# Seven of 32 zero regions in packets of 14 KiB, with a wider zero tile and the room for it, in a decode attention and FFN backward kernel

## Chip, cores and metric

One core of one Trainium2 chip. The metric is device time in microseconds, the median of several executions.

## The reference, cut to what matters

The reference computes one decode step of attention over the last 4096 keys of a long cache, a gated FFN, and the gradients of everything.

```python
W = min(4096, max(256, Sk // 4))              # 4096 of Sk = 32768
k = repeat(k_cache[:, :, Sk - W:, :], rep)    # B=2, Hkv=8, Dh=128, rep=4
v = repeat(v_cache[:, :, Sk - W:, :], rep)
p = softmax(q @ k.T * Dh ** -0.5)
h = x + (p @ v).reshape(B, 1, Hq * Dh) @ wo
out = h + (gelu(ln(h) @ w_gate) * (ln(h) @ w_up)) @ w_down
# returned: out and the gradients of x, k_cache, v_cache, wq, wo, w_gate, w_up, w_down
```

The gradients of the two caches are zero outside the last 4096 rows. These zeros are 32 regions (two tensors, two batches, eight heads) of 7 MiB each, 234.88 MB, and the kernel has to write them.

## The kernel before, where the change touches it

The zeros go out on GpSimd's queue from a u8 tile of 2048 columns. The DMA widens its bytes, so that a packet is 8 KiB of output (29376 packets for 234.88 MB on the page of the kernel before). (Three dots stand for further lines.)

```python
ZE = 2048
zt = const.tile([P, ZE], U8)
zero_regions = [...]                          # 32 regions of 7 MiB
ZPK = Z * DH // 2 // ZE
def zero_cast(i):
    dst, done = zero_regions[i].bitcast(F32), 0
    for rows, n in ZERO_PARTS.get(i, ((P, ZPK // P),)):
        ...
        nc.gpsimd.dma_start(out=..., in_=src.unsqueeze(1).to_broadcast([rows, n, ZE]))
...
nc.gpsimd.tensor_scalar(out=zt[:], in0=wq_sb[:, 0, 0:ZE // 2].bitcast(U8),   # after wq has landed
                        scalar1=0, scalar2=None, op0=ALU.mult)
for i in range(len(zero_regions)):
    zero_cast(i)
```

Attention of a batch runs over eight groups of heads. While VectorE and TensorE work on the products of group g (`m_unit`), TensorE transposes the K tile of group g+1 and computes its scores. There is one PSUM buffer for scores, below called the score bank:

```python
def s_unit(g, u, KT):
    if u == 0:
        S_ps[g] = ps_A.tile([P, NJ, REP], F32, tag="S", name="S_ps")   # pool with bufs=1
    ...
def softmax(g):
    S = S_ps.pop(g)
    ...                                                                # row maximum, negated
    ef = stA.tile([P, NJ, REP], F32, tag="ef", name="ef", bufs=1)
    ee = stA.tile([P, NJ, REP, 2], BF16, tag="ee", name="ee")
    nc.vector.tensor_tensor(out=ef[:], in0=S[:], in1=negm..., op=ALU.add)          # L394
    nc.scalar.activation(out=ef[:], in_=ef[:], func=ACT.Exp)                       # L395
    nc.vector.tensor_copy(out=ee[:], in_=ef[:].unsqueeze(3)...)                    # L396
    nc.vector.tensor_copy(out=eT[:]..., in_=ef[:]...)                              # L398
    nc.vector.reduce_sum(out=lsum[:, 0, ...], in_=ef[:]..., axis=AX.X)             # L400
```

In the lines of the profile PE is TensorE, DVE is VectorE, ACT is ScalarE, POOL is GpSimd, and SP is SyncE, which issues the loads and stores.

## Time and profile before

| | kernel before |
|---|---|
| the six executions known before the prediction | median 792.12 us, 791.67 to 796.31 |
| all 111 executions of this study | median 792.63, mean 793.5; 77 under 793.5, 11 at 798 or over |
| span of the profiled execution | 797.6 us |

The kernel ran again later (run e1); its profile there has a span of 790.2 us, and I use that one, called "the usual run" below, to compare with. The DMA rate in its forty slices of the span:

```profile
GB/s 364 420 417 421 419 426 427 422 430 427 429 422 418 426 423 423 426 424 430 429 428 428 429 427 426 429 422 428 428 428 430 423 422 421 424 419 423 422 381 367
```

The last two slices read 381 and 367 GB/s, where the profile that the prediction shows has 236 and 356. In a usual run the DMA engines work to the end.

### The profile page before, as it was taken

To read this page: it belongs to the slowest core of one execution; us is meant where nothing else is said; L and a number is where in the kernel's file an instruction comes from. 1 tells how busy PE (TensorE), PEld (TensorE's weight loads), DVE (VectorE), ACT (ScalarE), POOL (GpSimd) and SP (SyncE) were. 2 spreads that over 40 slices of the span, in tenths; PEclk is the share of its full clock that TensorE was granted. 3 is DMA by queue.
4 is the path that set the end of the run, shared out by engine and by line. 5 is a ranking of instruction groups with operands and counts; after the bars stand their busy time and mean duration, and the time that the engine had idled before them with its cause. 6 is when DMAs were issued, how large, how long until landed. Compare 5 with 4: busy or idle time off the path is not lost.

```text
span 797.6 us, 12388 instructions
## 1 busy us (share of the span) xinstructions
PE 563.4 (71%) x5032; PEld 302.5 (38%) x5096; DVE 474.0 (59%) x1161; ACT 280.9 (35%) x406; POOL 40.5 (5%) x58
## 2 busy tenths in 40 slices
PE   3899997787687998830837969988697733681072
PEld 3655653445555554410415444534242210220020
DVE  1699998137434898750821386755636944992093
ACT  1534330135245342100201343635443641682063
POOL 4300000000000000000000000000000000000000
PEclk9999999777699999885966868955586785996577
DMA  8999999999999999999999999999999999999968
GB/s 367 417 418 423 417 426 428 422 429 428 427 421 420 424 424 426 425 425 431 427 429 429 427 428 426 427 424 429 428 426 431 422 421 422 422 420 422 421 236 356
DMA packets 40986, 332.44 MB, mean 417 GB/s; under 512 B 2000, under 2 KB 2016, under 8 KB 2144
## 3 DMA queue, kind: packets, MB, share of 16 engines
q0 software_dynamic: 29376, 234.88, 77.0%
q1 hardware_dynamic: 11540, 96.75, 49.4%
q8 instruction: 40, 0.66, 0.3%
q10 hardware_dynamic: 12, 0.01, 0.2%
q14 instruction: 18, 0.15, 0.0%
HBM read 49.30 MB, written 282.33 MB: 416 GB/s over the span
## 4 chain that ended last, share of the span: by engine, by line
PE 22%; DMA 14%; DVE 8%; ACT 4%; issue 2%; SPq 1%; ACTq 0%; DVEq 0%
DMA out_dram<-mem 12%; PE ps_gr L713 3%; ACT mem L93 3%; PE ps_tb L240 3%; PE VT_ps L642 3%; PE ps_g L822 2%; DVE mem L91 2%; PE dP_ps L651 2%; DMA mem<-in_A_x_dram 2%; DVE junk L586 2%; PE ps_gq L793 1%; PE d_ln_ps L770 1%; PE attn_ps L516 1%; PE d_ln_ps L571 1%; DVE mem L733 1%
## 5 line engine op out<-in xcount | busy, mean ns | idle before, releaser
L408 DVE TENSOR_TENSOR mem<-mem,ee 128x512 bf16<-128x512 bf16 x512 | 181.0, 422 | 41.9 <-PE KT_ps L364 30.7
L419 PE MATMUL M_ps<-mem 128*128 128x512 bf16 x468 | 135.2, 390 | 9.2 <-DVE mem L408 6.1
L93 ACT CAST mem<-ps_g 128x512 bf16<-128x512 f32 x128 | 74.2, 585 | 88.9 <-PE ps_g L822 82.9
L822 PE MATMUL ps_g<-mem 128*128 128x512 bf16 x250 | 81.1, 417 | 21.4 <-DVE mem L91 14.0
L366 ACT COPY mem<-KT_ps 128x1024 bf16<-128x1024 bf16 x64 | 63.2, 1013 | 82.3 <-PE KT_ps L364 78.3
L91 DVE CAST mem<-ps_g 128x512 bf16<-128x512 f32 x128 | 82.6, 687 | 7.1 <-ACT mem L93 5.1
L364 PE MATMUL KT_ps<-ident_bf,mem 128*128 128x128 bf16 x512 | 45.9, 233 | 32.8 <-DMA mem<-in_A_k_cache_dram 29.5
L113 POOL DMA_DIRECT2D out_dram<-zt x38 | 32.4, 997 | 665.1 <-DMA out_dram<-zt 664.8
L240 PE MATMUL ps_tb<-ident_bf,mem 128*128 128x128 bf16 x480 | 56.3, 251 | 9.9 <-DMA mem<-in_B_w_gate_dram 3.2
L419 PEld LDWEIGHTS <-mem 128*128 128x128 bf16 x512 | 43.5, 99 | 48.3 <-issue 14.4
L822 PEld LDWEIGHTS <-mem 128*128 128x128 bf16 x256 | 26.0, 103 | 76.3 <-issue 57.0
L93 ACT COPY mem<-ps_tb 128x512 bf16<-128x512 bf16 x44 | 25.8, 585 | 74.9 <-PE ps_tb L240 70.1
L240 PEld LDWEIGHTS <-mem 128*128 128x128 bf16 x480 | 37.5, 128 | 35.5 <-issue 30.8
L364 PEld LDWEIGHTS <-mem 128*128 128x128 bf16 x512 | 34.5, 104 | 40.3 <-DMA mem<-in_A_k_cache_dram 30.0
L642 PE MATMUL VT_ps<-ident_bf,mem 128*128 128x128 bf16 x512 | 47.2, 241 | 2.9 <-ACT mem L93 1.1
L642 PEld LDWEIGHTS <-mem 128*128 128x128 bf16 x512 | 37.0, 108 | 28.1 <-issue 21.2
L651 PE MATMUL dP_ps<-mem 128*128 128x512 bf16 x114 | 41.1, 437 | 4.6 <-ACT mem L93 4.5
L93 ACT COPY mem<-VT_ps 128x1024 bf16<-128x1024 bf16 x31 | 31.7, 1022 | 35.2 <-PE VT_ps L642 34.0
L91 DVE COPY mem<-ps_tb 128x512 bf16<-128x512 bf16 x44 | 18.7, 424 | 42.0 <-PE ps_tb L240 40.6
L713 PE MATMUL ps_gr<-mem 2*128 2x512 bf16 (+1 forms) x78 | 33.6, 496 | 12.8 <-DVE mem L733 7.4
L261 PE MATMUL ps_rows<-ident_bf,mem 128*128 128x128 bf16 x4 | 1.1, 287 | 58.0 <-DVE mem L260 58.0
L91 DVE CAST mem<-ps_gr 128x512 bf16<-128x512 f32 (+1 forms) x38 | 24.8, 656 | 27.6 <-PE ps_gr L713 27.6
(242 smaller groups left out, 631.7 us busy)
## 6 DMA issues: line engine op xcount, KB each, us to landing
out_dram<-zt POOLq DMA_DIRECT2D x31, 7168.0 KB, 165.0
out_dram<-mem SPq DMA_DIRECT2D x36, 1024.0 KB, 28.9
mem<-in_A_k_cache_dram SPq DMA_DIRECT2D x16, 1024.0 KB, 23.1
mem<-in_A_v_cache_dram SPq DMA_DIRECT2D x16, 1024.0 KB, 22.5
out_dram<-mem SPq DMA_DIRECT2D x5, 1792.0 KB, 18.9
out_dram<-zt POOLq DMA_DIRECT2D x1, 5040.0 KB, 124.0
mem<-in_A_wq_dram SPq DMA_DIRECT2D x1, 4096.0 KB
mem<-in_A_wo_dram SPq DMA_DIRECT2D x1, 4096.0 KB, 31.4
```

Of the source, the lines that this page charges most:

```text
L91: nc.vector.tensor_copy(out=out, in_=in_)
L93: nc.scalar.copy(out=out, in_=in_)
L113: nc.gpsimd.dma_start(out=dst[done * ZE:(done + rows * n) * ZE].rearrange("(p k e) -> p k e", p=rows, k=n), in_=src.unsqueeze(1).to_broadc ...
L240: nc.tensor.transpose(out=ps[:, a, :], in_=src_block(a), identity=ident_bf[:])
L364: nc.tensor.transpose(out=KT_ps[:, jj, :], in_=Kt[b, g][:, u * 8 + jj, :], identity=ident_bf[:])
L366: nc.scalar.copy(out=KT[:], in_=KT_ps[:])
L408: nc.vector.tensor_tensor(out=pk[:, :, i, :].rearrange("p j (d t) -> p j d t", t=2), in0=Kb[:, j0:j0 + pk_j, :].rearrange("p j (d t) -> p ...
L419: nc.tensor.matmul(out=M_ps[:], lhsT=Vt[b, g][:, j, :], rhs=pk[:, jj, :, :].rearrange("p i d -> p (i d)"), start=(j == 0), stop=(j == NJ - 1))
L642: nc.tensor.transpose(out=VT_ps[:, jj, :], in_=Vt[b, g][:, a * 8 + jj, :], identity=ident_bf[:])
L651: nc.tensor.matmul(out=dP_ps[:, c, :], lhsT=dOpad[:, w0:w0 + P], rhs=VT[:, c * 4:(c + 1) * 4, :].rearrange("d a k -> d (a k)"), start=(i = ...
L713: nc.tensor.matmul(out=ps[:, :n], lhsT=lhsT_fn(k), rhs=rhs_fn(k), start=True, stop=True)
L822: nc.tensor.matmul(out=ps[:, a2, :], lhsT=lhs_bf[:, jp * P:(jp + 1) * P], rhs=rhs_bd[:, ap * 2 + a2, gq * 4:(gq + 1) * 4, :].rearrange("q ...
```

## The change

The intent is to save time in the seven regions written while no load or store runs, by fewer packets, of 14 KiB. This needs a zero tile of 3584 columns, and the other edits make its 1536 bytes per partition free.

```diff
-    ZE = 2048
+    ZE = 3584
     zt = const.tile([P, ZE], U8)
-    ZPK = Z * DH // 2 // ZE
+    ZE_BIG = (4, 5, 6, 17, 18, 19, 20)
     def zero_cast(i):
+        ze = ZE if i in ZE_BIG else 2048
+        zpk = Z * DH // 2 // ze
...
-    dqT_hb = small.tile([P, HQ, B], BF16)
...
-                ef = stA.tile([P, NJ, REP], F32, tag="ef", name="ef", bufs=1)
+                ef = S
...
+             tc.tile_pool(name="mid", bufs=1) as mid:
-            dO2 = small.tile([P, NOR], F32, name=f"dO2_{b}", tag="dO2")
+            dO2 = mid.tile([P, NOR], F32, name=f"dO2_{b}", tag="dO2")
-            dq_f32 = small.tile([P, HQ], F32, name=f"dq_f32_{b}", tag="dq_f32")
+            dq_f32 = mid.tile([P, HQ], F32, name=f"dq_f32_{b}", tag="dq_f32")
-            nc.scalar.activation(out=dqT_hb[:, :, b], in_=dq_f32[:], func=ACT.Copy, scale=SCALE)
...
-            nc.tensor.matmul(out=d_ln1_ps[:]..., lhsT=dqT_hb[:, h, :], ...)
+            nc.tensor.matmul(out=d_ln1_ps[:]..., lhsT=dqT_bf[:, h::HQ], ...)
```

More of the change, by code (lines that the diff above doesn't have):

```diff
@@ L99 @@
     dVv = out_3[:, :, Z:, :].rearrange("b g (p j) d -> p b g j d", p=P)
-    ZE = 2048
+    ZE = 3584
     zt = const.tile([P, ZE], U8)
     zero_regions = [o[b, g, 0:Z, :].rearrange("r d -> (r d)") for o in (out_2, out_3) for b in range(B) for g in range(HKV)]
-    ZPK = Z * DH // 2 // ZE
-    ZERO_PARTS = {i: ((4, 1), (15, 2), (2, 2), (15, 42), (12, 3), (P, 1), (16, 4)) for i in (30,)}
+    ZE_BIG = (4, 5, 6, 17, 18, 19, 20)
+    ZERO_PARTS = {30: ((4, 1), (15, 2), (2, 2), (15, 42), (12, 3), (P, 1), (16, 4))}
     def zero_cast(i):
         dst, done = zero_regions[i].bitcast(F32), 0
-        for rows, n in ZERO_PARTS.get(i, ((P, ZPK // P),)):
-            src = zt[0:rows * (P // rows):P // rows, :]
-            nc.gpsimd.dma_start(out=dst[done * ZE:(done + rows * n) * ZE].rearrange("(p k e) -> p k e", p=rows, k=n),
-                                in_=src.unsqueeze(1).to_broadcast([rows, n, ZE]))
+        ze = ZE if i in ZE_BIG else 2048
+        zpk = Z * DH // 2 // ze
+        for rows, n in ZERO_PARTS.get(i, ((P, zpk // P),)):
+            src = zt[0:rows * (P // rows):P // rows, 0:ze]
+            nc.gpsimd.dma_start(out=dst[done * ze:(done + rows * n) * ze].rearrange("(p k e) -> p k e", p=rows, k=n),
+                                in_=src.unsqueeze(1).to_broadcast([rows, n, ze]))
             done += rows * n
-        assert done == ZPK
+        assert done == zpk
     dh2_x = at(OFF_XR, [98, D], BF16, "xr")
@@ L505, in middle @@
         with tc.tile_pool(name="ps_W", bufs=2, space=PSUM) as ps_W, \
-             tc.tile_pool(name="ps_B", bufs=1, space=PSUM) as ps_B:
+             tc.tile_pool(name="ps_B", bufs=1, space=PSUM) as ps_B, \
+             tc.tile_pool(name="mid", bufs=1) as mid:
             attn_ps = ps_B.tile([B, D], F32)
@@ L769, in use_q @@
         def use_q(h, wqT_h):
-            nc.tensor.matmul(out=d_ln1_ps[:].rearrange("b a p -> b (a p)"), lhsT=dqT_hb[:, h, :],
+            nc.tensor.matmul(out=d_ln1_ps[:].rearrange("b a p -> b (a p)"), lhsT=dqT_bf[:, h::HQ],
                              rhs=wqT_h[:].rearrange("d a p -> d (a p)"), start=(h == 0), stop=(h == HQ - 1))
```

## The prediction

> **What bounds the kernel now.** I read the DMA rows of the page first, then the queue table, then the chain of work that ended last, then single stretches.
>
> The page's slices and its queue table:
>
> ```profile
> DMA  8999999999999999999999999999999999999968
> GB/s 367 417 418 423 417 426 428 422 429 428 427 421 420 424 424 426 425 425 431 427 429 429 427 428 426 427 424 429 428 426 431 422 421 422 422 420 422 421 236 356
> DMA packets 40986, 332.44 MB, mean 417 GB/s; under 512 B 2000, under 2 KB 2016, under 8 KB 2144
> q0 software_dynamic: 29376, 234.88, 77.0%
> q1 hardware_dynamic: 11540, 96.75, 49.4%
> ```
>
> The DMA engines run at 417 to 431 GB/s in all slices but the first and the last two. q0 is the zero fill: 234.88 MB in 29376 packets is 8.0 KB each (2048 bytes of the u8 zero tile, widened to 8192 bytes of output). q1 is everything useful, 96.75 MB. So the zeros are 71% of the bytes and fill whatever the loads and stores leave free. A first reading is "bandwidth-bound: any gain in the rate is a gain in time". The two low slices, 758 to 797 us, speak against that. The chain of work that ended last there:
>
> ```profile
> 638.17 30.30 DMA out_dram<-mem
> ...
> 690.00 26.33 DMA out_dram<-mem
> 716.35 40.67 DMA out_dram<-mem
> 757.99 1.10 issue
> 759.09 2.37 DVE mem L271 x2
> ```
>
> The busy table of stretches (length, busy us of PE, PEld, DVE, ACT and POOL, granted clock, DMA share, GB/s):
>
> ```profile
> 628.00:758.00 130.00, 57.95 (x184) 18.58 (x185) 70.56 (x109) 53.75 (x93) 2.04 (x3) 0.75 1.16 422
> ...
> 762.00:770.00 8.00, 6.71 (x21) 2.27 (x20) 6.69 (x11) 5.46 (x10) 0.00 (x0) 0.74 0.56 210
> 770.00:776.00 6.00, 5.19 (x19) 1.70 (x18) 5.53 (x10) 5.13 (x10) 0.00 (x0) 1.00 0.26 109
> ```
>
> The last of the four dK/dV jobs can build its block-diagonal operand (L271) only at 757.99 us, when a store that had 40.67 us to run has landed: the scratch rows of that builder lie in the bytes of a store staging buffer. From there 39.6 us follow to the end (2.4 us of build, some 24 us of matmuls and evictions, then the last 4 MiB of stores), and in them the DMA engines are largely empty (210, then 109 GB/s). What sets the 757.99 us is the store queue. From 628 to 757 us it moved 25.99 MB in 129 us, 201 GB/s, while the zeros took 28.35 MB[...]. The zeros' last bytes (0.88 MB) go out between 757 and 769 us, after that point. So the end is "useful stores at half rate, then a fixed tail", and before 628 us a chain of compute and load latencies, with the zeros as filler. A faster zero stream alone does not move this chain while it still outlasts 758 us.
>
> The zero stream alone, in a stretch of 16 us without loads (208 to 224 us, DMA view):
>
> ```profile
> DMA packets 850, 6.84 MB, mean 428 GB/s; under 512 B 15, under 2 KB 15, under 8 KB 15
> q0 software_dynamic: 849, 6.82, 114.1%
> ```
>
> 428 GB/s over 16 engines is 26.7 GB/s each: 8192 B every 306 ns.
>
> [...] the row maximum from PSUM (L380) took 289 ns, the row sum of the same shape from SBUF (L400) 377 ns.
>
> **The change part by part.**
>
> *Packets.* A region is 7168 KiB: 896 packets of 8 KiB (56 per engine) become 512 of 14 KiB (32 per engine). [...] 56 x 306 = 17.14 us; [...] Saved: 0.11 us a region, 0.8 us over seven. It is a 0.7% faster stream in 15% of the time.
>
> Which stretches are they? Eight zero DMAs are in flight, and issue number k+8 follows the landing of k, so the GpSimd timeline dates them:
>
> ```profile
> 13.76 5.37 POOL L301 TENSOR_SCALAR zt<-mem 128x2048 uint8<-128x2048 uint8 x1 [10.04 <-DMA mem<-in_A_wq_dram]
> 19.44 7.60 POOL L113 DMA_DIRECT2D out_dram<-zt  x8 [0.31 <-POOL zt L301]
> ...
> 148.41 0.90 POOL L113 DMA_DIRECT2D out_dram<-zt  x1 [20.59 <-DMA out_dram<-zt]
> 171.31 0.90 POOL L113 DMA_DIRECT2D out_dram<-zt  x1 [22.00 <-DMA out_dram<-zt]
> 188.88 0.90 POOL L113 DMA_DIRECT2D out_dram<-zt  x1 [16.67 <-DMA out_dram<-zt]
> 206.78 0.90 POOL L113 DMA_DIRECT2D out_dram<-zt  x1 [17.00 <-DMA out_dram<-zt]
> ```
>
> Regions 4, 5, 6 land at 171, 189 and 207 us, and 17 to 20 between 424 and 495 us: the two "middle" stages. Only the first third of region 4 shares the engines, with two K tiles not needed before attention of batch 1. The V loads come at 213 us, the first gradient store at 501 us. So no load or store on the chain is slowed.
>
> *Zero tile.* 3584 columns instead of 2048: 5.37 x 1.75 = 9.4 us on GpSimd, so the zeros start 4 us later, near 23.5 us. The load queue then holds the first K and V tiles and uses the engines alone; it empties some 4 us earlier and the zeros catch up. Bytes are only reordered: 0 us. Attention of batch 0 is bound by VectorE (18.6 to 19.6 busy us in each 20 us from 40 to 120 us), so earlier K and V tiles don't help it.
>
> *Room for the tile.* The other edits pay for 1536 bytes per partition. The f32 exponentials now stay in the PSUM scores: four VectorE instructions and one ScalarE one per group, 16 groups. [...] +0.15 us a group, 2.4 us in all as an upper estimate. In the trace these instructions overlap (row sum and casts start 0.14 to 0.20 us apart, for durations of 0.22 to 0.37), so I take a quarter, +0.6 us. Holding the score bank longer costs nothing: the next scores are written after products that need the same exponentials. One ScalarE copy per batch (dqT_hb) goes; it is off the chain. The weight load of dqT_bf with a stride is 32 loads of 79 ns beside the matmuls: 0. Two small tiles change pool: 0.
>
> Sum: the 0.8 us of the zeros land mostly in the empty tail, of which I count 0.3; the softmax gives back perhaps 0.6. That is +0.3 us. Against this stands that such a tile was worth making room for, which speaks for some gain that I do not see in the profile; for it I take off 0.8 us. 792.1 becomes 791.6 us.
>
> **The rivals.**
>
> 1. *The saving counts in full.* The page's DMA row is full nearly to the end, and an unprofiled run is shorter by 5.5 us than the profiled 797.6, so its tail may be tighter. Then 0.8 us and no softmax cost: 791.3. Against: the hole of 762 to 776 us.
> 2. *The softmax in PSUM is exposed.* VectorE is over 93% busy in attention of batch 0, and each later stage hangs on it. Then +2.4 us: 794.5 at most. Against: the overlap of these instructions.
> 3. *Larger packets hold up transfers at the edges.* A 2 KiB load issued at 402 us beside 8 KiB zeros took 12.8 us, and the K tile issued at 343.7 us kept PE waiting until 377.6: [...] For a single such wait, 1 to 3 us: 793 to 795. Against: the regions were chosen clear of these loads.
> 4. *Fewer packets let a lagging engine catch up*, so that a K load or the store at 716 us lands some us sooner: 788 to 790. I see no row that shows it.
>
> **Range and chances.** The runs before lie at 791.67 to 796.31, most within 0.7 us. Rivals 2 and 3 reach up to 794 or 795, 4 down to 788; 789.3 to 793.8 should hold it. Two per cent is 15.8 us, twenty times the saving worked out: 0.01 for either side.
>
> **What would show it right or wrong.** Right: q0 has 29376 - 7 x 384 = 26688 packets; regions 5, 6 and 17 to 20 land 0.1 us sooner each (17.0 us apart, some 431 GB/s in these stretches); the zero tile takes 9 us and zeros start near 23.5 us; the chain still ends in the store wait before L271, with 39 to 40 us after it; zeros end after that wait. Wrong: a rate above 434 GB/s in the big regions, longer waits of PE for K or of the row load before the middle stage, VectorE rows of the softmax longer by over 60 ns each with attention later by over 1 us, or zeros that end before the last store wait, in which case the saving does reach the end.

## More of the kernel before

The order in which instructions stand on each engine is not the order of the source: the build's scheduler sets it.

## The result, and the profile after

The changed kernel took 800.07 us (median of 10, 791.86 to 801.05, mean 798.8; one under 793.5, eight at 798 or over). The kernel before took 792.19 us beside it (20 executions, mean 793.1). The ratio is 1.0072, 95% interval 1.0046 to 1.0098: within 2%, but slower. A ratio is always the mean time of one kernel's fast runs over that of the other's in the same rounds, so it is not quite the ratio of the medians that I quote. The prediction had said 791.6 us, and 793.8 at most.

The page of the changed kernel, its rate by slice and its two main queues:

```profile
GB/s 366 419 421 422 419 427 426 429 425 432 424 424 419 422 426 424 427 425 429 428 431 432 430 430 424 430 419 430 429 429 426 425 420 421 425 420 422 423 185 350
...
q0 software_dynamic: 26688, 234.88, 76.0%
q1 hardware_dynamic: 11540, 96.75, 47.0%
```

The zero queue has exactly the 26688 packets that the prediction worked out. The 23rd and 24th slices, from 440 to 480 us, in a stage of large packets, read 430, no outlier. What stands out is the hole near the end: 185 GB/s in the slice before the last.

GpSimd's timeline of the changed kernel (start, us, engine, line, operation, and in brackets the idle time before it):

```profile
13.55 9.27 POOL L301 TENSOR_SCALAR zt<-mem 128x3584 uint8<-128x3584 uint8 x1 [9.81 <-DMA mem<-in_A_wq_dram]
23.13 7.06 POOL L114 DMA_DIRECT2D out_dram<-zt  x8 [0.31 <-POOL zt L301]
...
441.39 0.90 POOL L114 DMA_DIRECT2D out_dram<-zt  x1 [21.07 <-DMA out_dram<-zt]
...
494.39 0.90 POOL L114 DMA_DIRECT2D out_dram<-zt  x1 [16.81 <-DMA out_dram<-zt]
```

The tile takes 9.27 us and the zeros start at 23.13 us. From 441.39 to 494.39 us three regions of large packets land: 53.0 us. In the usual run the same three took 53.4:

```profile
441.71 0.90 POOL L113 DMA_DIRECT2D out_dram<-zt  x1 [16.73 <-DMA out_dram<-zt]
...
495.11 0.90 POOL L113 DMA_DIRECT2D out_dram<-zt  x1 [16.44 <-DMA out_dram<-zt]
```

Over all profiles (the kernels told below among them), nine with large packets there took 53.1 us in the mean, and eleven with small ones 53.3. This is 0.06 us a region. One of the eleven, e8, took 53.1 too; the other ten lie above all nine. The saving is real and is worth 0.4 us over seven regions.

The end of the chain that ended last. First the usual run of the kernel before, then the changed kernel:

```profile
633.27 30.65 DMA out_dram<-mem
...
681.45 29.09 DMA out_dram<-mem
710.55 39.38 DMA out_dram<-mem
750.90 1.10 issue
752.01 2.36 DVE mem L271 x2
```

```profile
643.66 30.54 DMA out_dram<-mem
...
693.94 28.15 DMA out_dram<-mem
722.10 36.40 DMA out_dram<-mem
...
759.47 1.10 issue
760.57 2.37 DVE mem L272 x2
```

It is the same chain in both, so the prediction had the right one. It enters it at 643.66 instead of 633.27 us, 10.4 us late, and leaves it 8.6 us late. A stretch of the tail, 770 to 776 us, shows what the lateness does. The DMA view of the usual run, then of the changed kernel:

```profile
DMA packets 347, 2.56 MB, mean 426 GB/s; under 512 B 36, under 2 KB 36, under 8 KB 36
```

```profile
DMA packets 0, 0.00 MB, mean 0 GB/s; under 512 B 0, under 2 KB 0, under 8 KB 0
```

When the chain is on time, the last stores follow the last zeros without a gap. When it is late, the zeros run out first, and the engines stand idle until the last job has something to store. The slices of the page say the same.

Where does the lateness come from? The table gives start times, in us, of one instruction in each stage: L391's copy of the softmax of the last group of batch 0, and of the first, seventh and last groups of batch 1; then the issue of the first dK/dV store and of the first store of the last job. The kernels e6 to e18 are told below.

| profile | last group, batch 0 | first group, batch 1 | 7th group, batch 1 | last group, batch 1 | first dK/dV store | last job's first store | span |
|---|---|---|---|---|---|---|---|
| before, usual run (e1) | 120.3 | 253.8 | 338.4 | 382.9 | 631.9 | 766.1 | 790.2 |
| before, slow run | 119.9 | 254.1 | 338.9 | 386.0 | 636.8 | 773.7 | 797.6 |
| changed kernel | 129.2 | 258.2 | 345.5 | 393.1 | 642.3 | 775.2 | 799.3 |
| e6, exponentials in PSUM only | 124.4 | 254.1 | 343.8 | 386.8 | 634.9 | 768.6 | 792.4 |
| e16, the same in PE's old order | 122.2 | 254.0 | 344.3 | 387.8 | 636.6 | 773.4 | 797.1 |
| e18, PE's new order, SBUF | 124.4 | 254.6 | 339.7 | 387.4 | 636.7 | 773.5 | 797.5 |
| e17, changed kernel in PE's old order | 129.5 | 258.5 | 350.9 | 392.7 | 641.4 | 775.0 | 798.9 |
| e12, packets, late tile, SBUF | 126.0 | 254.3 | 337.1 | 382.5 | 631.5 | 765.6 | 789.8 |
| e7, a flawed test (below) | 121.2 | 254.6 | 349.7 | 399.0 | 654.3 | 774.8 | 798.5 |

Three things can be read from it. First, between the last group of batch 0 and the first of batch 1 there is slack: e12 enters 5.7 us late and leaves 0.5 us late. The changed kernel enters 8.9 us late, and 4.5 us remain. Second, it loses another 2.7 us by the seventh group of batch 1, and 3.1 us at the load of the last K tile, where PE waited 28.2 us rather than the 25.5 of the usual run. The slow run of the kernel before waited 28.8 there, so this last part need not come from the change. Third, the end follows the first dK/dV store, but in a steep step. Over all 20 profiles, a first store up to 634.9 us goes with a span of at most 792.7 us, and one from 636.6 us with 797.1 or more; two stores at 636.1 us gave 794.7 (e15) and 796.7 (e3). It hardly grows from there, since at 654.3 us it is 798.5. A chain that is 5 us late costs 7 us, one that is 22 us late costs 8.

So single executions lie more often near one of two levels than between them (of all 252, 94 under 793.5 us, 95 at 798 or over), and a kernel that is a little later reaches the upper one more often. A part of the change is to be judged by the shift of the whole set of executions.

Of the 8.9 us, 7.3 arise at one place: from the fifth group's copy (82.5 us) to the sixth's (102.7 us) the changed kernel took 20.2 us, the usual run 12.9. PE waited 2.7 us there for a K tile. The stretch from 88 to 101 us in the usual run and in the changed kernel (length, busy us of PE, its weight loads, DVE, ACT and POOL, granted clock as a share of TensorE's full speed, DMA share, GB/s):

```profile
88.00:101.00 13.00, 12.57 (x173) 7.74 (x171) 12.76 (x42) 4.91 (x7) 0.90 (x1) 1.00 1.31 419
```

```profile
88.00:101.00 13.00, 10.83 (x95) 5.10 (x97) 6.03 (x18) 0.59 (x1) 0.35 (x1) 0.61 1.24 422
```

The granted TensorE clock was 0.61 there, against 1.00. Large packets play no part: the first starts at 139.8 us. Of e3, the same kernel without them, the profile has the clock at 1.00 in this stretch and enters only 3.7 us late. So one profile of a kernel can hold some us that another has not, and no run here tells whether the low clock causes such a delay or follows from the wait.

### The profile page after: what moved, and what is told of

The parts are those of the page before. It is cut to its first block, busy times and chain, and to the rows that moved or that the text cites. A ratio compares the mean times of both kernels' runs of the same rounds, so it can differ in the third digit from the quotient of the medians.

```text
span 799.3 us, 12391 instructions
## 1 busy us (share of the span) xinstructions
PE 562.2 (70%) x5032; PEld 300.0 (38%) x5096; DVE 475.1 (59%) x1161; ACT 278.3 (35%) x404; POOL 43.2 (5%) x58
## 3 DMA queue, kind: packets, MB, share of 16 engines
q0 software_dynamic: 26688, 234.88, 76.0%
## 5 line engine op out<-in xcount | busy, mean ns | idle before, releaser
L419 PE MATMUL M_ps<-mem 128*128 128x512 bf16 x468 | 137.4, 392 | 15.9 <-DVE mem L408 7.0
L364 PE MATMUL KT_ps<-ident_bf,mem 128*128 128x128 bf16 x512 | 43.8, 230 | 35.7 <-DMA mem<-in_A_k_cache_dram 30.9
L91 DVE COPY mem<-VT_ps 128x1024 bf16<-128x1024 bf16 x33 | 23.1, 701 | 28.4 <-PE VT_ps L642 27.8
```

What stands on the lines that cost most here:

```text
L91: nc.vector.tensor_copy(out=out, in_=in_)
L364: nc.tensor.transpose(out=KT_ps[:, jj, :], in_=Kt[b, g][:, u * 8 + jj, :], identity=ident_bf[:])
L419: nc.tensor.matmul(out=M_ps[:], lhsT=Vt[b, g][:, j, :], rhs=pk[:, jj, :, :].rearrange("p i d -> p (i d)"), start=(j == 0), stop=(j == NJ - 1))
```

## The experiments

The runs came in five lots; each was measured beside the kernel before on the same chip. "Mean" is the mean of all executions of the run.

**e1: the kernel before, unchanged.** It asks whether the profiled run before was a usual one.

> The kernel before, unchanged, to learn what its usual execution looks like: the one profiled first took 799.28 us, while the median is 792.2. All theories: 792 us, ratio 1.000. If the profiled execution is a usual one (790 to 792 us span), its trace should show where some 7 us of the first profile came from: either a shorter path up to the first dK/dV store (636.83 us before), or a shorter tail (39.6 us from the last builder's wait to the end).

Six executions at 791.52 to 792.05 us, span 790.2. The profile that I predicted from was not a usual one.

**e2: the change without its packets; e3: with the wide tile but small packets; e4: the whole change with a prompt start of the zeros.**

```diff
 e2 (from the changed kernel)
-    ZE = 3584
+    ZE = 2048
-    ZE_BIG = (4, 5, 6, 17, 18, 19, 20)
+    ZE_BIG = ()
 e3 (from the changed kernel)
-        ze = ZE if i in ZE_BIG else 2048
+        ze = 2048
 e4 (from the changed kernel)
+    nc.vector.memset(zt[:, 2048:ZE].bitcast(U32), 0)      # at the start
-                nc.gpsimd.tensor_scalar(out=zt[:], in0=wq_sb[:, 0, 0:ZE // 2].bitcast(U8),
+                nc.gpsimd.tensor_scalar(out=zt[:, 0:2048], in0=wq_sb[:, 0, 0:1024].bitcast(U8),
```

> Only the edits that make room (exponentials kept in PSUM, small tiles moved, no dqT_hb); zero tile 2048 wide, all packets 8 KiB. Theory A (VectorE reads the exponentials from PSUM, attention of batch 0 and all loads behind it come late, a K tile is missed): 798 to 801 us, the VectorE casts at 421 and 284 ns instead of 289 and 222. Theory B (the wider tile takes 9.3 us, zeros start 4 us late): 792 us. Theory C (14 KiB packets crowd out loads): 792 us.

> The changed kernel with all packets of 8 KiB: room edits and the 3584 wide zero tile (zeros start near 23 us), no big packets. Theory A: 798 to 801 us. Theory B: 798 to 801 us, and a PE wait for K(0,6) near 88 us. Theory C: 792 us.

> The changed kernel with 14 KiB packets in the same seven regions, but only the first 2048 columns of the zero tile are made after wq has landed; the other 1536 are set by VectorE at the start, so that zeros start near 19.4 us as before. Theory A: 798 to 801 us. Theory B: 790 to 792 us. Theory C: 798 to 801 us.

e2 took 796.9 us (mean 797.0), e3 798.7 (mean 797.8), e4 800.04 (mean 799.2). None of the 18 executions was under 793.5. The kernel without one large packet is slow too, so most of the loss seems to lie in the edits that made the room. Beside their own runs of the kernel before, e2 (ratio 1.0025, 0.9981 to 1.0068) and e3 (1.0035, 0.9993 to 1.0076) are not clear of noise, and e4 barely is (1.0049, 1.0003 to 1.0095). A prompt start does not bring the whole change back.

**e5 and e7: the whole change with its exponentials in SBUF again, with the late tile and the prompt tile. Both are flawed.**

```diff
-                ef = S
+                ef = at(OFF_R1, [P, NJ, REP], F32, "ef")
```

> The changed kernel with one edit undone: the exponentials lie in SBUF again (in a scratch stretch of the big tile that is free then); 14 KiB packets, wide tile and late start of the zeros stay. The built order of PE in attention of batch 0 is again that of the kernel before. Theory A (the exponentials in PSUM are the loss): 791 to 793 us, G waits gone, the load of w_up issued near 129.5 us as before. Theory B (late start of the zeros): 796 us or more. Theory C (big packets, which e4 left at 800.0 against 796.9 of e2): 795 to 796 us.

> As e5, with the zeros also started at 19.4 us (the other 1536 columns of the tile set by VectorE at the start). Theory A: 791 to 792 us, the 14 KiB packets worth 0 to 0.8 us. Theory B: 791 to 792, and at least 3 us below e5. Theory C: 795 to 796 us, as e5.

They took 800.22 and 800.38 us. In batch 1 that place belongs to the product buffers, so each softmax had to wait for them: the rows for the second half were loaded at 411 and 418 us, against 398 in the usual run. They say nothing on the packets. But e7 gives the last row of the table: 22 us of lateness end as 8.

**e6: the kernel before with only the exponentials in PSUM; e8: the same, with the K transposes held behind matmuls of earlier groups.**

```diff
 e6 (from the kernel before)
-                ef = stA.tile([P, NJ, REP], F32, tag="ef", name="ef", bufs=1)
+                ef = S
 e8 adds, around the transposes of K
+                with tc.issue_after(behind) if behind is not None else ExitStack():
```

> The kernel before with one edit: the exponentials stay in the PSUM scores; everything else as before. Theory A: 796 to 797 us as e2, w_up issued near 135 us, the long ScalarE wait for the K transposes (7 us) as in e2. Theories B and C: 792 us.

> As e6, with the K transposes held behind the products of the group before, so that PE does not run ahead of the loads; the exponentials still in PSUM. Inside theory A: if the loss is the order that the scheduler made of PE's work, 792 to 794 us and w_up issued before 132 us; if it is the slower VectorE rows themselves (421 and 284 ns for 289 and 222), 796 to 797 us as e6.

e6 took 797.5 us (mean 797.7, none under 793.5), ratio 1.0052 (1.0014 to 1.009). This one line brings most of the loss. Why is not told by it, because the line also changes the build: PE's instructions in attention stand in another order (the lists that e18 and e16 use below split it into 404 stretches of one kind, and that of the kernel before into 432), and the transposes of K bunch up. e8 was to undo that but made a third order, and took 801.5 us; it is inconclusive.

**e9, e10, e11: the packets with PE's old order.** The exponentials stay in SBUF. The room comes from other small tiles, after which PE's order is that of the kernel before but for one matmul. e9 has the large packets and the late tile, e10 the large packets and a prompt tile, e11 the late wide tile and small packets.

```diff
 e9 (from the kernel before, with the packets of the change)
-            lsum = small.tile([P, 4, HQ], F32, name="lsum", tag="l4")
+            lsum = small.tile([P, HQ], F32, name="lsum", tag="lsum")
+            l4 = stA.tile([P, 2, DH], F32, tag="oPK", name="l4", bufs=1)...   # fourfold copy, shares a buffer
-    dOT_f32 = small.tile([P, NBH], F32)
+    dOT_f32 = small.tile([P, HQ], F32)
...                                           # dO2, dO_sel, prod4, dq_f32 to the pool "mid"; no dqT_hb
```

> 14 KiB packets in the same seven regions and the late, wide tile, but the exponentials in their own SBUF tile as before; the room comes from small tiles alone (row sums, two score tiles), and the built order of PE is that of the kernel before up to one matmul. In e5 and e7 the scratch stretch chosen for the exponentials turned out to be used by the product buffers of batch 1, so their 800 us do not speak for or against packets. Theory A2 (the loss of the changed kernel is the order that PE got when the exponentials moved to PSUM): 790.5 to 792.5 us, first dK/dV store issued at 631 to 633 us. Theory C (packets): 796 us or more, first store after 636 us.

> As e9, with the zeros started at 19.3 us. Theory A2: 790.5 to 792.5 us, equal to e9 within 0.5. Theory B (late start costs something of its own): 1 us or more below e9. Theory C: as e9, 796 us or more.

> As e9 with all packets of 8 KiB: the late wide tile alone. All theories but B: 792 us; the packets of e9 are then worth (e9 minus e11): A2 says -0.8 to 0, C says +3 to +8. Theory B: 796 us or more.

e9 took 800.48 us (8 executions; two under 794, six over 800), e10 793.47, e11 793.15. That looked as if large packets with a late start were a second cause. With six to eight executions at two levels it may as well be chance, so I did not believe it.

**e12 to e15: the same question with more executions.** e12 is e9 again and e15 is e11 again. e13 has large packets only in the four late regions, e14 only in the three early ones.

```diff
 e13                                          | e14
-    ZE_BIG = (4, 5, 6, 17, 18, 19, 20)       | -    ZE_BIG = (4, 5, 6, 17, 18, 19, 20)
+    ZE_BIG = (17, 18, 19, 20)                | +    ZE_BIG = (4, 5, 6)
```

> Unchanged from e9 (packets of 14 KiB in seven regions, wide tile that is zeroed late, exponentials in SBUF), with more runs, because single runs of one kernel lie at about 792 or at about 800 us and e9's 8 runs can't tell a shift from chance. If the seven regions of large packets are a second cause of their own, most runs again lie near 800 us (median above 798) and the profile, if it falls there, shows a first store later than the 633.6 us of e9's fast profile. If e9 was chance, the median is 792 to 794.5, as for the kernel before and for e11.

> As e12, but 14 KiB only in regions 17 to 20, which are written between the last row load and the first stores. If large packets cost through transfers that come after regions 17 to 20, median about 799 to 800 us; if they cost through the loads after regions 4 to 6, or e9 was chance, 792 to 794.5 us.

> As e12, but 14 KiB only in regions 4 to 6, which are written just before the V and K loads of the second half. If those loads are what large packets hold up, median about 799 to 800 us; otherwise 792 to 794.5 us.

> Unchanged from e11 (same late wide tile, exponentials in SBUF, all packets 8 KiB), as the control of the other three with as many runs. Expected 792 to 794.5 us by both theories; if it too shows most runs near 800 us, it is the late start of the zeros and not the packets that costs.

e12 took 793.02 us (mean 795.0), e13 796.06 (mean 796.7), e14 795.64 (mean 795.7), e15 795.54 (mean 795.6). The median of e9 did not come back, so much of it was chance (e9 and e12 together: 14 executions, mean 797.0). All 32 executions with large packets and SBUF exponentials (e9, e10, e12 to e14) have a mean of 796.3 us, the 12 with small packets (e11, e15) one of 795.1. With some 3 us between executions, 1.2 us is about one standard error. No effect of the packets on the whole time is resolved, in either direction. These kernels as a set (44 executions, mean 796.0, 14 under 793.5) are later than the kernel before (793.5), by less than those with the exponentials in PSUM. Which of the other edits they owe that to, I did not separate.

**e16, e17, e18: order or PSUM?** Here every PE instruction of attention is chained to the one that stood before it in a recorded order. e16 is e6 in the old order (by the count in its expectation, four places of 875 differ). e18 is the kernel before in e6's order. e17 is the whole change in the old order.

```diff
+            for run in PE_ORDER[b].split():      # recorded from the other kernel
+                for ins in next_of_kind(run):
+                    tc.add_manual_dep(ins, last.name, mybir.DependencyInfo(mybir.DependencyClass.NoSync, ...))
+                    last = ins
```

> The kernel before with the exponentials in the score bank, as e6, but with PE's instructions in attention chained into the order that they had in the kernel before (4 of 875 stretches differ; e6: a fifth of them). If the order is what costs in e6, mean back from e6's 797.7 to about 793.5 us, like the kernel before. If the longer DVE operations on PSUM and the longer hold of the score bank cost, it stays at 797 to 798 us, with the row load for the second half issued at about 402 us as in e6 and not at 398.

> The counterpart: the kernel before with its exponentials in SBUF, but PE's instructions in attention chained into e6's order (K transposes bunched ahead of the group's end). If the order costs, mean about 797 to 798 us; if PSUM's durations and the hold of the bank cost, about 793.5 us. If both this and e16 lie between, each carries a part.

> The whole changed kernel (packets of 14 KiB in seven regions, late wide tile, exponentials in PSUM) with PE's instructions in attention chained into the order of the kernel before. If the order is the main cause, mean falls from the 798.8 of the changed kernel to 794 to 796 us, which is what the kernels with the same zeros and SBUF exponentials took (e9, e10, e12 to e14: 796.3 in the mean); if not, about 799 us.

e16 took 800.05 us (22 executions, mean 798.9, none under 793.5), ratio 1.0065 (1.0044 to 1.0086). e18 took 795.65 us (14 executions, mean 796.1), ratio 1.0027 (1.0003 to 1.0051). e17 took 800.0 us (12 executions, mean 799.4), ratio 1.0064 (1.0038 to 1.0089).

PE's order as the main cause falls. With the old order the PSUM kernel is as slow as with the new one, and so is the whole change. The new order alone, with SBUF exponentials, costs about half as much; I had thought that it was the cause. What else the one line brings is left, and the trace of e16 shows one way. PE's waits in the profile of the usual run from 253 to 346 us, that is over the first seven groups of batch 1 (what waited, for whom: us in total, times, longest):

```profile
PE M_ps L419 <- DVE mem L408: 2.7, 4, 0.9
PE S_ps L374 <- issue: 1.5, 1, 1.5
...
PE S_ps L374 <- ACT mem L366: 0.4, 2, 0.2
```

And in e16, then in e17 (their line numbers are shifted: L437 issues the matmuls, L403 is the row sum):

```profile
PE S_ps L437 <- DVE lsum L403: 6.2, 5, 1.5
```

```profile
PE S_ps L437 <- DVE lsum L403: 7.1, 6, 1.5
```

The usual run has no wait for the row sum at all, and neither has the slow run of the kernel before. In e16 PE waits five times, 6.2 us in all, before it may write new scores, because the last reader of the old exponentials in the score bank is the row sum. From the first to the seventh group, e16 takes 90.3 us and the usual run 84.7, by the table: 5.6 us more. e17 takes 92.4. The nine profiles with PE's old order and the exponentials in an SBUF tile of their own (before, e1, e9 to e15) take 80.4 to 85.4.

The wait is shown; that the 5.6 us are its price is not. First, e16 restores the order of PE alone. In its group at 290 us, VectorE has 21 products between the row maximum and the next step of the softmax, where the usual run has 3. Second, the granted clock from 279 to 293 us was 0.63 in e16 and 0.88 in the usual run. Third, in the order that the build chooses for PSUM this wait is nearly gone (0.3 us in e6, and in the changed kernel), and the same groups take from 82.5 us (e3) over 86.7 (e2), 87.1 (e4) and 87.3 (changed kernel) to 89.8 (e6); the new order with SBUF (e18) takes 85.1. In that order PSUM's own part is not resolved: e2 and e6 have a mean of 797.4, e18 one of 796.1, and the difference has a standard error of 1.0.

All executions but those of the flawed e5 and e7 and of e8, by what the kernels have:

| kernels | executions | mean us | under 793.5 | 798 and over |
|---|---|---|---|---|
| before, with e1 | 111 | 793.5 | 77 | 11 |
| late wide tile, small packets, SBUF (e11, e15) | 12 | 795.1 | 4 | 3 |
| large packets, SBUF (e9, e10, e12, e13, e14) | 32 | 796.3 | 10 | 14 |
| PE's new order, SBUF (e18) | 14 | 796.1 | 2 | 5 |
| PSUM, small packets, prompt zeros (e2, e6) | 12 | 797.4 | 0 | 5 |
| the same in the old order (e16) | 22 | 798.9 | 0 | 15 |
| room edits, late wide tile, small packets (e3) | 6 | 797.8 | 0 | 4 |
| the whole change with prompt zeros (e4) | 6 | 799.2 | 0 | 5 |
| the whole change (after) | 10 | 798.8 | 1 | 8 |
| the whole change in the old order (e17) | 12 | 799.4 | 0 | 10 |

No kernel beats the kernel before.

## Why the prediction was wrong

1. **The bound.** The chain was right (stores, the builder's wait, a fixed tail; from the builder's wait to the end 39.3 us in the usual run and 39.8 after). What failed is that I took the hole of 762 to 776 us for a feature of the kernel. The usual run moves 426 GB/s from 770 to 776 us. The profile's 797.6 us against executions at 792 should have told me so: other profiled runs differ from their device time by 1.7 to 1.9 us (790.2 and 792.05 in e1), not by 5.5. I saw the difference and put it down to the profiler.
2. **The packets.** Right in kind, and over-estimated by about half: 0.06 us a region where I had 0.11. The 0.11 was my estimate: the trace before has 306 ns for 8 KiB and does not show what a larger packet takes. The regions landed 17.7 us apart (17.8 with small packets), not the 17.0 that I gave as a sign. The 0.4 us of seven regions are too small to see in the time.
3. **The zero tile.** The times were right (9.27 us; zeros from 23.13 us). "Bytes are only reordered: 0 us" was too simple. e12, with the late tile, is 5.7 us late at the end of attention of batch 0, and e10, with a prompt tile, isn't late there (120.2 us). But the slack before batch 1 takes such a delay up. In the changed kernel's profile most of the lateness was that of the one group after 82.5 us (above).
4. **The exponentials in PSUM. This is the step that failed:** the term of +0.6 us, 2.4 at most, for the softmax, with "Holding the score bank longer costs nothing: the next scores are written after products that need the same exponentials." The kernels with this line in PSUM measured 4.8 us above the kernel before, twice the ceiling. The reason given is wrong: the products need `ee` and `eT`, the casts; the row sum comes after those, and no product waits for it. The scores of the next group can be ready to be written before it has run, and e16 and e17 show PE waiting for it, 6.2 and 7.1 us in batch 1. The changed kernel as built shows only 0.3 us of that wait there: its PE order had moved with the line. The prediction had not thought of that either, and the new order costs 2.6 us with the exponentials in SBUF (e18 against the kernel before). So it is shown that the term was too small, and that the bank is waited for in the old order; which path carries the loss in the changed kernel stays open. The durations, for which I had only an estimate that the trace before did not show (0.15 us a group), account for less. The softmax rows of the usual run and of the changed kernel (minimum/median/maximum in ns):

```profile
L394 DVE TENSOR_TENSOR ef<-S_ps,negm x16: 281/284/292, 25.0 to 383.3; 128x128 f32<-128x128 f32 x16
L395 ACT ACTIVATE ef<-ef x16: 309/310/311, 25.3 to 383.6; 128x128 f32<-128x128 f32 x16
L396 DVE CAST ee<-ef x16: 282/284/294, 28.2 to 384.2; 128x256 bf16<-128x256 f32 x16
L398 DVE CAST mem<-ef x16: 216/218/221, 28.4 to 384.4; 128x128 bf16<-128x128 f32 x16
L400 DVE TENSOR_REDUCE lsum<-ef x16: 366/372/376, 28.5 to 384.5; 128x4 f32<-128x128 f32 x16
```

```profile
L394 DVE TENSOR_TENSOR S_ps<-S_ps,negm x16: 292/294/299, 25.1 to 393.5; 128x128 f32<-128x128 f32 x16
L395 ACT ACTIVATE S_ps<-S_ps x16: 262/274/288, 26.7 to 393.9; 128x128 f32<-128x128 f32 x16
L396 DVE CAST ee<-S_ps x16: 415/421/426, 28.2 to 394.4; 128x256 bf16<-128x256 f32 x16
L398 DVE CAST mem<-S_ps x16: 281/284/285, 28.6 to 394.7; 128x128 bf16<-128x128 f32 x16
L400 DVE TENSOR_REDUCE lsum<-S_ps x16: 282/284/288, 28.8 to 394.9; 128x4 f32<-128x128 f32 x16
```

   By the medians a group pays 10 - 36 + 137 + 66 - 88 = +89 ns, 1.4 us over 16 groups, inside my upper estimate of 2.4. PSUM exponentials cost 4.8 us by the executions (e2, e6 and e16: 34 with a mean of 798.3, against 793.5). How much of that is the hold, how much the durations, the orders of PE and VectorE, the granted clock and the knock-on delays, the runs do not divide; to move the exponentials to a PSUM bank of their own would take the hold away, and was not run.
5. **The rest.** The strided weight loads took 81 ns each, against 79 without the stride. The smaller edits cost nothing that six executions each can show: e2 has them all in addition to PSUM and took 797.0 us in the mean, e6 with PSUM alone 797.7.
6. **The sum.** Taking 0.8 us off because "such a tile was worth making room for" had no row of the profile behind it, and should not have been there.

Of the rivals, the second was nearest, with too low a ceiling (794.5): it counted durations only. The third, larger packets that hold up transfers, is not borne out. The parts do not add up: 4.8 us for PSUM and 2.5 us for the rest (the 44 executions at 796.0, whose room edits are partly others) would make 800.8, and the whole change took 798.8 to 799.4. The step in the table would explain this: once the chain is late enough to fall to the upper level, more lateness costs little.

What stays open: why the step lies between 634.9 and 636.6 us and why it is so steep. In the slow run of the kernel before, stores from 600 to 775 us waited 28.9 us for earlier stores, against 23.1 in the usual run. This is a difference that the profiles show and not yet a cause. The same holds for what tips one and the same program to one level or the other.

## What to carry to other kernels

Before you read a profile as the kernel's, compare its span with the unprofiled times: a profile 5 us above the median is that of a slower execution. When a tile moves into a buffer that its producer needs back, ask for the last reader of that buffer and not for the first. When a one-line edit lets the build reorder the engines, compare their orders and the granted clock too, before a wait in one trace is called the cause. And where executions fall to two levels, compare the share at each level with enough executions: e9's median of 800.5 over eight became 793.0 over six.
